# Chunk 0 of a delta-rule attention kernel: where the unread TensorE products stand, at which steps the next chunk's keys are turned, and when the betas are copied

## The chip, the cores and the metric

The kernel runs on one core of a Trainium2 chip. A core has five engines that run side by side, each working through its own list of instructions in order: TensorE (PE in the profile; its weight loads are listed as PEld), VectorE (DVE), ScalarE (ACT), GpSimd (POOL) and SyncE (SP, which here only issues DMAs). Engines wait for one another through semaphores. The metric is the device time of one execution in microseconds (us). A run's time is a little longer than the span that the profile shows, which goes from the first instruction to the last.

## The reference: a delta rule, then a two-layer network

The inputs are q, k and v of shape (4 batches, 8 heads, 768 tokens, 48), and beta of shape (4, 8, 768). Cut to what matters, the reference is:

```python
k_n = k / (np.linalg.norm(k, axis=-1, keepdims=True) + 1e-06)
for t in range(S):
    y[:, :, t] = np.einsum('bhd,bhde->bhe', q[:, :, t], state)
    v_old = np.einsum('bhde,bhd->bhe', state, kt)
    state = state + bt[:, :, :, None] * np.einsum('bhd,bhe->bhde', kt, vt - v_old)
# x: y as (3072 tokens, 384)
h = x @ w_in                       # 384 -> 2048
g = h * (1.0 / (1.0 + np.exp(-h)))
out = g @ w_out                    # 2048 -> 384
```

Every token reads a 48 x 48 state per head, takes out what the state already holds for its key, and adds what is missing. The result goes token by token through a network with a SiLU between two products.

## The kernel before

The 768 tokens are cut into six chunks of 128, and each chunk into halves of 64. Within a chunk the sequential rule becomes products of matrices: the keys' scores against each other, the inverse of a triangular matrix made of them, and products with values, queries and state. All 32 pairs of batch and head are worked on together. The network of the chunks that are done runs on TensorE between the steps of the next chunk, so that TensorE is nearly always busy; only chunk 0 has nothing to run beside it. This case is about the first 50 us, in which chunk 0 is prepared.

**Who sets the order.** The program is one long list in the source. `pin(op)` ties every instruction behind the one before it on the same engine, so each engine runs its instructions in the order in which the source makes them. DMAs on SP are chained by `in_line`. Later loads of weights are held until TensorE reaches certain instructions: `pin` counts TensorE's instructions, and `loads` names the counts.

**The steps of chunk 0, in the order of TensorE.** A "turn" transposes the keys (`turn(c, b, 0, ...)`, b being the batch) or the queries (`turn(c, b, 1, ...)`) of one batch on TensorE with four 128 x 128 transposes (L510); ACT or DVE copies the result out of PSUM (L520 for queries, L524 for keys on ACT, L522 for keys on DVE). `score` multiplies turned keys with turned keys, or with turned queries, in 16 small products of 64 x 64 (L539, two matmul records for each); the copies of its result are L554 on ACT and L557 on DVE. `first_score(b)` are the key scores, `first_queries(b)` the query scores. `beta_of(c)` transposes the betas of one chunk on TensorE (L361) and copies them out on ACT (L364). `diagonal_blocks` copies the blocks of the key scores that are to be inverted (L554 on ACT, L560 on POOL), and `turn_diagonal` transposes them on DVE (L578).

**The chain on DVE.** `norm_steps(0)` computes the inverse lengths of the keys in small steps of DVE (L403 to L426); the step at L420 multiplies them by the betas of chunk 0. `invert_first` then inverts 16 x 16 blocks: a first step (L697) and 15 pairs of steps (L705, L709), each of which is a `next(inv)` in a loop over `n`, and two transposes at the end (L716, L720). The `joins` put the blocks together: `corner` (L743 on TensorE, L750 on DVE), `turned` (L759), `straight` (L772) and `merge_half` (L832). The first product of `corner` waits for L716, and L750 stands behind L720 on DVE.

**The unread products.** `busy(n)` puts n products of the zeroed state with the identity matrix on TensorE (L347, 128 x 384, two matmul records for each product). Nobody reads them. With an instruction and `Sync` given, the first of them waits for that instruction. `busy` and the copies of scores share three PSUM banks in turn.

**Around the change.** Behind the key scores stand the two query turns of batches 0 and 1, one `busy`, the query scores of batch 0, three `busy`, the query scores of batch 1, the transposes of the betas of chunks 1 to 5, two `busy`, the query turns and the query scores of batches 2 and 3. ACT then narrows the first piece of `w_in` (`begin`, L233 and L234). In the loop over `n` stand one `busy` behind each of the steps 0, 1, 2, 4 and 8 and one behind step 15, and the turns of chunk 1's keys at the steps 10, 12, 14 and 15. These turns take their PSUM banks from `M`, which has two, so the third turn waits for ACT's copy (L524) of the first, and the fourth for that of the second. The copies go into `stage`, where the diagonal blocks lay before. After this loop come the joins.

Of the kernel before, what the change touches and what calls it, by code (L numbers as in the profile page):

```python
# [19 lines left out]
def kernel(  # L20
# [37 lines left out]
    A, CC, M = deque(("a0", "a1", "a2")), deque(("c0", "c1", "c2")), deque(("m0", "m1"))  # L58
    kept_banks = {tag: banks.tile([P, 512], FP32, name=f"pb_{tag}", tag=tag) for tag in CC}

    def bank(room, name):

        tag = room[0]
        room.rotate(-1)
        return kept_banks.get(tag) or banks.tile([P, 512], FP32, name=name, tag=tag)

    NoSync, Sync = mybir.DependencyClass.NoSync, mybir.DependencyClass.Sync

    def behind(later, earlier, how=NoSync):

        tc.add_manual_dep(
            later.ins, earlier.ins.name,
            mybir.DependencyInfo(how, mybir.DependencyReason.DATA), reason="order",
        )
# [3 lines left out]
    def pin(op):  # L78

        engine = op.ins.engine  # L80
        if engine in pins:
            behind(op, pins[engine])
        pins[engine] = op
        if engine in tensor[:1]:
            begun[0] += 2 if op.ins.is_transpose else 4
            while loads and begun[0] >= loads[0][0]:
                paced(*loads.popleft()[1:])
        return op
# [254 lines left out]
    def busy(n=1, after=None, how=NoSync, wide=DM):  # L343

        for _ in range(n):
            pw = bank(CC, "pw")
            done = pin(nc.tensor.matmul(  # L347
                pw[:, 0:wide], lhsT=ident[:],
                rhs=states[0][:].rearrange("p u a w -> p (u a w)")[:, 0:wide], start=True, stop=True,
            ))  # L350
            tensor.append(done.ins.engine)
            if after is not None:
                behind(done, after, how)
                after = None
# [4 lines left out]
    def beta_of(c):  # L359
        pb = bank(A, "pb")  # L360
        pin(nc.tensor.transpose(  # L361
            pb[:, 0:BH], beta_fm[:, c].rearrange("n s t -> n (s t)"), ident[0:BH, 0:BH]
        ))
        pin(nc.scalar.activation(  # L364
            out=beta_tok[:, c, :].rearrange("p (n e) -> p e n", e=2),
            in_=pb[:, 0:BH].rearrange("p (e n) -> p e n", e=2), func=ACTF.Copy,
        ))
# [19 lines left out]
    def add_squares(c, b):  # L387

        pin(nc.vector.tensor_reduce(
            out=sums[c][:, b * H : (b + 1) * H], in_=squared[c, b], axis=AX.X, op=ALU.add  # L390
        ))
# [92 lines left out]
    def kq_room(c, b):  # L484

        if c != 1:
            kqs[c, b] = turned_kq[:, b].rearrange("p j a t -> p a j t")
        elif b % HB == 0:
            both = stage[:].rearrange("p (u j a t) -> p u a j t", u=B, a=NP, j=2)
            for u in range(HB):  # L490
                kqs[c, b + u] = both[:, b + u]
# [11 lines left out]
    def turn(c, b, j, room, by_vector=False):  # L503

        if j == 0:
            kq_room(c, b)
        src, kq = (kbufs[c % 2], queries[c] if c < 2 else None)[j][:, b], kqs[c, b]
        pt = bank(room, "pt")
        for p in range(NP):
            pin(nc.tensor.transpose(  # L510
                pt[:, p * C : (p + 1) * C], src[:, p].rearrange("p e w -> p (e w)"), ident[:]
            ))
        ptv = pt[:].rearrange("p (a t) -> p a t", a=NP)
        if j == 1:
            if by_vector:
                pin(nc.vector.tensor_scalar(
                    out=kq[:, :, j, :], in0=ptv, scalar1=-1.0, scalar2=None, op0=ALU.mult
                ))
            else:
                pin(nc.scalar.mul(kq[:, :, j, :], ptv, -1.0))  # L520
        elif by_vector:
            pin(nc.vector.tensor_copy(out=kq[:, :, j, :], in_=ptv))  # L522
        else:
            pin(nc.scalar.copy(kq[:, :, j, :], ptv))  # L524

    def score(c, b, js, rooms, evacuate):

        g, u = b // HB, b % HB
        if (c, g) not in aps:
            aps[c, g] = {}  # L530
        for j in js:
            if j not in aps[c, g]:
                aps[c, g][j] = work.tile([P, HB, H, W], FP32, name=f"ap{j}", tag=f"ap{j}", bufs=2)
        ap, kq, n = aps[c, g], kqs[c, b], len(js)
        pa = [bank(room, f"pa{e}") for e, room in enumerate(rooms)]
        for p in range(NP):
            for e, hf in ((0, 0), (1, 1), (0, 1), (1, 0)):
                rows, half = slice(W * e, W * e + D), slice(W * hf, W * (hf + 1))
                pin(nc.tensor.matmul(  # L539
                    pa[e][half, p * n * W : (p + 1) * n * W], lhsT=kq[rows, p, 0, half],  # L540
                    rhs=kq[rows, p, js[0] : js[-1] + 1, half], start=True, stop=True,
                ))
        for e in range(2):
            of = pa[e][:, 0 : NP * n * W].rearrange("p (a j t) -> p a j t", a=NP, j=n)
            for i, j in enumerate(js):
                evacuate(j, e, ap[j][:, u, e::2, :], of[:, :, i, :])
# [17 lines left out]
    def diagonal_blocks(c, g, engines):  # L564

        if g == 0:
            room = stage if c == 0 else sum_room
            diagonals[c] = room[:, 0 : BH * T].rearrange("p (n t) -> p n t", t=T)
        for j, by in enumerate(engines):
            rows, cols = slice(T * j, T * (j + 1)), slice(T * (j % 2), T * (j % 2 + 1))  # L570
            by(
                diagonals[c][rows, HH * g : HH * (g + 1)],
                aps[c, g][0][rows].rearrange("s u h t -> s (u h) t")[:, :, cols],
            )
# [740 lines left out]
    def first_score(b):  # L1315

        def evacuate(j, e, to, of):
            (by_dve if e else by_act)(to, of)

        score(0, b, (0,), (A, CC), evacuate)  # L1320
# [14 lines left out]
    first_score(1)  # L1335
    first_score(2)
    first_score(3)
    diagonal_blocks(0, 0, (by_pool, by_pool, by_act, by_act))
    diagonal_blocks(0, 1, (by_act, by_act, by_act, by_act))
    add_squares(0, B - 1)  # L1340
    beta_of(0)

    def first_queries(b):

        def evacuate(j, e, to, of):
            by_act(to, of)

        score(0, b, (1,), (A, CC), evacuate)
# [4 lines left out]
    load_v(0)  # L1353
    for b in range(2):
        turn(0, b, 1, M)
    busy(1)
    for _ in norm_steps(0):
        pass
    first_queries(0)
    busy(3)  # L1360
    first_queries(1)
    step = step_of[0]
    of_step = blocks[0][2].rearrange("p s t -> p (s t)")[:, 0 : T * T : T + 1]
# [34 lines left out]

    for n in range(Q):
        done = next(inv)  # L1400
        if n in (0, 1, 2, 4, 8):
            busy(1, done, Sync)
        if n == 10:
            turn(1, 0, 0, M)
        if n == 12:
            turn(1, 1, 0, M)
        if n == 14:
            turn(1, 2, 0, M)
        if n == 15:
            busy(1, done, Sync)  # L1410
            turn(1, 3, 0, M)
    corner, turned, straight = next(inv)
    pin(nc.gpsimd.memset(slab, 0.0))

# [192 lines left out]
    for c in range(1, NCH):  # L1607
# [5 lines left out]
        for word in chunks[c].split():  # L1613
            what, n = word[0], int(word[1:] or 1)
# [55 lines left out]
```

## Time and profile before

| | |
|---|---|
| median of 3 runs | 642.54 us (642.02 to 643.44) |
| the profiled execution's own time | 641.09 us |
| its span | 638.9 us |
| mean granted TensorE clock | 0.987 of full |
| TensorE busy | 621.8 us, 97% of the span |
| VectorE busy | 396.8 us, 62% |
| ScalarE busy | 222.2 us, 35% |
| GpSimd busy | 94.0 us, 15% |

The page divides the span into 40 slices of 16 us. A timeline row gives start, duration, engine, source line, operation, result and operands, size, and how many like instructions it merges; in brackets is the engine's idle time ahead of it and who ended that. The chain is the work that ended last, followed back from the end; "issue" in it is time in which the engine waited for nothing that the profile shows. A row of the table of windows gives a stretch of time, its length, and for each engine the busy time and the number of records in it, then the granted clock of TensorE, the busy share of the DMA engines and GB/s.

### The profile page before, as it was taken

What the parts mean: (1) busy time and instruction counts of PE and PEld (TensorE: products, weight loads), DVE (VectorE), ACT (ScalarE), POOL (GpSimd) and SP (SyncE); (2) the same over time, 40 slices, a digit from 0 to 9 for tenths busy, and PEclk for the clock granted to TensorE, in tenths of its full rate; (3) what the DMA queues carried; (4) which work ended last, traced back from release to release, by engine and by line L of the source; (5) the groups of instructions that cost most, each with busy time, mean ns of one, the idle gap of its engine ahead of it and who ended that gap; (6) DMA issues with size and microseconds to landing.
All of it is one profiled execution on the core that took longest, in us unless ns stands there. A gap on an engine that the chain in (4) does not pass through costs nothing.

```text
span 638.9 us, 21371 instructions
## 1 busy us (share of the span) xinstructions
PE 621.8 (97%) x9406; PEld 546.5 (86%) x9406; DVE 396.8 (62%) x900; ACT 222.2 (35%) x511; POOL 94.0 (15%) x101
## 2 busy tenths in 40 slices
PE   6979999999999999999999999999999999999997
PEld 4678778656799989989989989989889989989997
DVE  6866879999676974546974545975455964112112
ACT  5456883323351122451122451122451122441120
POOL 5223741335020020020020020020002000000000
PEclk9779999999999999999999999999999999999999
DMA  9646606350367450459150359242353133010101
GB/s 174 130 128 176 201 16 149 100 98 4 81 117 169 77 99 12 104 96 193 27 96 16 81 123 161 54 86 26 64 114 79 26 73 37 16 39 1 26 0 26
DMA packets 136940, 52.60 MB, mean 82 GB/s; under 512 B 108672, under 2 KB 130432, under 8 KB 136848
## 3 DMA queue, kind: packets, MB, share of 16 engines
q1 hardware_dynamic: 136512, 51.09, 39.0%
q8 instruction: 74, 1.21, 0.8%
q10 hardware_dynamic: 336, 0.15, 0.1%
q14 instruction: 18, 0.15, 0.1%
HBM read 39.09 MB, written 9.96 MB: 77 GB/s over the span
## 4 chain that ended last, share of the span: by engine, by line
PE 95%; ACT 1%; issue 1%; DMA 1%; DVE 0%; SPq 0%; POOL 0%; POOLq 0%
PE phid L1072 40%; PE px L1189 17%; PE py L1189 13%; PE po L1116 5%; PE pa L539 3%; PE pb_c L866 3%; PE pb_c L854 2%; PE pyc L945 2%; PE pb_c L1116 2%; PE pb_c L886 1%; PE pyc L932 1%; PE pb_c L347 1%; PE px L808 1%; PE py L808 1%; PE pt L510 1%
## 5 line engine op out<-in xcount | busy, mean ns | idle before, releaser
L1072 PE MATMUL phid<-xT,w_in 128*128 128x256 f32 x1152 | 257.1, 381 | 0.2 <-DVE xT L919 0.2
L1072 PEld LDWEIGHTS phid<-xT,w_in 128*128 128x128 f32 x1152 | 216.4, 190 | 30.2 <-issue 0.9
L1082 ACT ACTIVATE gT<-phid 128x512 f32<-128x512 f32 x88 | 52.4, 597 | 142.2 <-PE phid L1072 135.5
L1170 DVE TENSOR_TENSOR sums_of_g<-gT 128x384 f32<-128x384 f32 (+1 forms) x60 | 30.3, 527 | 66.1 <-ACT gT L1082 55.8
L656 DVE SCALAR_TENSOR_TENSOR rank<-g,step,x 128x31 f32<-128x31 f32 (+15 forms) x124 | 49.8, 401 | 22.2 <-DMA g<-blocks 18.7
L1189 PE MATMUL px<-sums_of_w,sums_of_g 128*128 128x192 f32 x320 | 56.6, 329 | 0.0
L1189 PE MATMUL py<-w_out,sums_of_g 128*128 128x192 f32 x320 | 56.2, 328 | 0.0
L1189 PEld LDWEIGHTS px<-sums_of_w,sums_of_g 128*128 128x128 f32 x320 | 52.2, 190 | 0.4
L1189 PEld LDWEIGHTS py<-w_out,sums_of_g 128*128 128x128 f32 x320 | 52.3, 190 | 0.3
L661 DVE TENSOR_TENSOR x<-x,rank 128x31 f32<-128x31 f32 (+15 forms) x124 | 42.5, 343 | 4.3
L477 POOL TENSOR_TENSOR vf<-vf,n_slot 128x768 f32<-128x768 f32 x10 | 14.8, 1492 | 175.0 <-DMA vf<-in_v_dram 120.5
L554 ACT COPY xT<-pyc 48x128 f32<-48x128 f32 (+2 forms) x126 | 32.7, 260 | 1.7
L498 DVE STREAM_TRANSPOSE kq<-stage 128x512 f32<-128x512 f32 x28 | 28.3, 1116 | 5.1 <-DMA xT<-part 3.4
L1189 PE MATMUL py<-w_out,gT 128*128 128x192 f32 x160 | 29.1, 330 | 0.0
L1200 DVE TENSOR_TENSOR o<-o,kept 128x192 f32<-128x192 f32 (+1 forms) x29 | 11.5, 421 | 27.1 <-ACT kept L1197 27.1
L1189 PE MATMUL px<-w_out,gT 128*128 128x192 f32 x160 | 27.9, 327 | 0.0
L1189 PE MATMUL px<-sums_of_w,gT 128*128 128x192 f32 x160 | 27.8, 327 | 0.0
L560 POOL COPY g<-x 64x256 f32<-64x256 f32 x4 | 5.0, 1243 | 150.5 <-DVE x L664 150.5
L1189 PEld LDWEIGHTS px<-w_out,gT 128*128 128x128 f32 x160 | 26.5, 190 | 0.6
L1189 PEld LDWEIGHTS py<-w_out,gT 128*128 128x128 f32 x160 | 26.1, 190 | 0.5
L891 DVE TENSOR_TENSOR state<-state,pb_c 128x384 f32<-128x384 f32 x22 | 11.2, 550 | 24.3 <-PE pb_c L886 24.2
L1189 PEld LDWEIGHTS px<-sums_of_w,gT 128*128 128x128 f32 x160 | 26.2, 190 | 0.1
(232 smaller groups left out, 941.0 us busy)
## 6 DMA issues: line engine op xcount, KB each, us to landing
vf<-in_v_dram SPq DMA_DIRECT2D x48, 96.0 KB, 2.9
out_dram<-o SPq DMA_DIRECT2D x42, 96.0 KB, 2.2
w_out<-in_moe_w_in_dram SPq DMA_DIRECT2D x4, 768.0 KB, 4.8
sums_of_w<-in_moe_w_out_dram SPq DMA_DIRECT2D x4, 768.0 KB, 4.6
kb<-in_k_dram SPq DMA_DIRECT2D x12, 192.0 KB, 4.2
kb<-in_k_dram SPq DMA_DIRECT2D x24, 96.0 KB, 4.1
raw<-in_moe_w_in_dram SPq DMA_DIRECT2D x3, 768.0 KB, 7.1
blocks<-ap SPq DMA_DIRECT2D x32, 64.0 KB, 1.9
```

The lines of the kernel that those rows point to most:

```text
L477: pin(nc.gpsimd.tensor_tensor(out=vf, in0=vf, in1=of, op=ALU.mult))
L498: pin(nc.vector.transpose(out=kqs[c, b][:, :, j, :].rearrange("p a (i m) -> p a m i", i=T), in_=src.rearrange("p a (m d) -> p a m d", d=D) ...
L539: pin(nc.tensor.matmul(pa[e][half, p * n * W : (p + 1) * n * W], lhsT=kq[rows, p, 0, half], rhs=kq[rows, p, js[0] : js[-1] + 1, half], sta ...
L554: return pin(nc.scalar.copy(to, of))
L656: pin(nc.vector.scalar_tensor_tensor(out=tv, in0=g[:, 0:m, m : m + 1].to_broadcast([P, m, n]), scalar=step[:, m : m + 1], in1=x[:, m : m + ...
L661: yield pin(nc.vector.tensor_tensor(out=x[:, 0:m, m:T], in0=x[:, 0:m, m:T], in1=tv, op=ALU.add))
L866: yield pin(nc.tensor.matmul(pz[rows, n * D : (n + 1) * D], lhsT=xis[g][rows, u * H + 2 * p + e, :], rhs=vfs[c][rows, hf, g * HB + u, p, : ...
L1072: pin(nc.tensor.matmul(ph[:, j * GT : (j + 1) * GT], lhsT=w_in[:, a, (2 * f + j) * P : (2 * f + j + 1) * P], rhs=xTs[c, hf][:, a, :], star ...
L1082: pin(nc.scalar.activation(out=hidden_of(c, hf, f), in_=ph[:], func=ACTF.Silu, scale=-0.5 if in_blocks(c) else 0.5))
L1116: pin(nc.tensor.matmul(pos[i][:, 0:DM], lhsT=hidden_of(0, hf, f // 2)[:, at : at + C], rhs=w_outs[f // HFF][:, f % HFF, :], start=(f == 0) ...
L1170: pin(nc.vector.tensor_tensor(out=sums_of_g[:, k, fs], in0=of[0], in1=of[1], op=op))
L1189: pin(nc.tensor.matmul(to, lhsT=at, rhs=quarter(f, *b) if isinstance(b, tuple) else sums_of_w[b][:, f], start=start and f == 0, stop=f == ...
```

## The change

Three things are moved, and nothing is added or taken away.

1. `beta_of(0)` stands ahead of the diagonal copies. On TensorE nothing changes by this; on ACT the copy of chunk 0's betas (L364) comes ahead of six copies of diagonal blocks (L554) instead of behind them.
2. The three `busy` between the query scores of batch 0 and batch 1 stand ahead of both, together with the one that was there.
3. In the loop of the inversion there is no `busy` behind the steps 0, 1, 2, 4, 8 and 15. There are two behind step 9, two behind step 11, one behind step 13 and one behind step 14. The turns of chunk 1's keys stand at the steps 6, 8, 10 and 12 instead of 10, 12, 14 and 15.

The number of `busy` is 15 before and after, and TensorE's instructions from `corner` on keep their places in its list.

```diff
+    beta_of(0)
     diagonal_blocks(0, 0, (by_pool, by_pool, by_act, by_act))
     diagonal_blocks(0, 1, (by_act, by_act, by_act, by_act))
     add_squares(0, B - 1)
-    beta_of(0)
...
     for b in range(2):
         turn(0, b, 1, M)
-    busy(1)
+    busy(4)
     for _ in norm_steps(0):
         pass
     first_queries(0)
-    busy(3)
     first_queries(1)
...
     for n in range(Q):
         done = next(inv)
-        if n in (0, 1, 2, 4, 8):
+        if n in (9, 11, 13):
+            busy(2 if n < 13 else 1, done, Sync)
+        if n in (6, 8, 10, 12):
+            turn(1, n // 2 - 3, 0, M)
+        if n == 14:
             busy(1, done, Sync)
-        if n == 10:
-            turn(1, 0, 0, M)
-        if n == 12:
-            turn(1, 1, 0, M)
-        if n == 14:
-            turn(1, 2, 0, M)
-        if n == 15:
-            busy(1, done, Sync)
-            turn(1, 3, 0, M)
```

## The prediction, made before the changed kernel was run

> **What bounds the kernel now.** The page comes first: its busy times, the slices and the chain.
>
> ```profile
> PE 621.8 (97%) x9406; PEld 546.5 (86%) x9406; DVE 396.8 (62%) x900; ACT 222.2 (35%) x511; POOL 94.0 (15%) x101
> PEclk9779999999999999999999999999999999999999
> PE 95%; ACT 1%; issue 1%; DMA 1%; DVE 0%; SPq 0%; POOL 0%; POOLq 0%
> ```
>
> TensorE is the chain for 95% of the span, and its clock is below full in slices 1 and 2 alone, 16 to 48 us. Behind that it has work without a break, so what is gained or lost ahead of about 50 us should reach the end unchanged. The second view is the chain in order of time, from chunk 0's diagonal copies to the joins.
>
> ```profile
> 15.78 0.49 ACT kq L520
> 16.32 0.36 PE pa L539
> 17.45 4.14 PE pb_c L347 x6
> 22.67 0.63 ACT ap L554 x2
> 26.40 0.27 PE pa L539
> 27.58 0.76 PE pb_c L347 x2
> 28.37 0.93 ACT w_in L233
> 29.30 0.95 ACT raw L234
> 31.52 0.60 ACT stage L524
> 33.47 0.44 PE pt L510 x4
> 33.90 0.14 PE pl L743 x2
> 35.61 0.25 issue
> 37.63 1.96 issue
> 42.07 1.09 issue
> ```
>
> Three unread products (six records, L347) stand between the first two query scores for 4.14 us, on the path. Each stage up to `corner` (L743, about 33.85) follows them. The third view is the table of windows, which tells why they are so slow.
>
> ```profile
> 5.32:8.73 3.41, 2.38 (x43) 1.55 (x42) 1.61 (x3) 1.45 (x3) 1.96 (x3) 1.00 0.91 155
> 12.15:15.56 3.41, 1.04 (x6) 0.42 (x4) 2.81 (x14) 3.33 (x6) 0.55 (x4) 1.00 1.12 293
> 15.56:18.97 3.41, 2.65 (x35) 1.93 (x36) 3.05 (x5) 1.82 (x5) 2.57 (x8) 0.50 0.86 124
> 18.97:22.39 3.42, 3.42 (x37) 1.74 (x35) 2.94 (x13) 0.00 (x0) 0.00 (x0) 0.50 0.97 258
> 36.04:39.45 3.41, 1.59 (x128) 1.48 (x122) 2.74 (x7) 1.62 (x5) 0.83 (x1) 1.00 0.61 162
> 42.87:46.28 3.41, 3.12 (x87) 3.05 (x87) 2.23 (x5) 2.24 (x4) 0.00 (x0) 0.50 0.91 273
> 48.00:50.00 2.00, 2.00 (x62) 1.92 (x60) 1.82 (x3) 0.59 (x2) 0.00 (x0) 0.57 0.05 11
> ```
>
> The clock is 1.00 up to 15.56, 0.50 to 22.39, and 0.50 again from 39.45; the 0.57 of the last row puts the second rise at 49.7. The two spells are 6.8 and 10.2 us, two and three times 3.41, and the falls lie 23.9 us apart, seven times 3.41: the clock changes on a grid of 3.41 us. A window with 1.04 us of work (30%) or 1.59 (47%) was followed by a fall, one with 2.38 (70%) was not. A cold window of 2.65 or of 3.12 us was not followed by a rise, one of 3.42 was.
>
> **The change part by part.** The timeline gives the prices (PE, ACT, DVE).
>
> ```profile
> 12.38 0.81 PE L347 MATMUL pb_c<-state,ident 128*128 128x384 f32 x2
> 17.38 2.93 PE L347 MATMUL pb_c<-state,ident 128*128 128x384 f32 x4
> 23.72 1.56 PE L347 MATMUL pb_c<-state,ident 128*128 128x384 f32 x4
> 22.52 0.31 PE L361 MATMUL pb<-ident,beta_fm 32*128 32x32 f32 x2
> 23.08 0.71 PE L361 MATMUL pb<-ident,beta_fm 32*128 32x32 f32 x3 [0.24 <-ACT ap L554]
> 25.11 1.04 PE L510 MATMUL pt<-ident,z 128*128 128x128 f32 x8
> 11.79 3.76 ACT L554 COPY stage<-ap 32x512 f32<-32x512 f32 x6
> 15.81 0.19 DVE L420 TENSOR_TENSOR nt<-nr,beta_tok 128x32 f32<-128x32 f32 x1 [0.41 <-ACT beta_tok L364]
> 24.18 0.29 DVE L709 TENSOR_TENSOR sums_of_w<-sums_of_w,rank 128x126 f32<-128x126 f32 x1
> 27.84 1.06 DVE L716 STREAM_TRANSPOSE sums_of_w<-sums_of_w 128x512 f32<-128x512 f32 x1
> 34.58 0.34 DVE L750 SCALAR_TENSOR_TENSOR sums_of_w<-pl,second,pick 64x128 f32<-64x128 f32 x1 [3.87 <-PE pb_c L743]
> ```
>
> Betas first: ACT does the same copies before the query turns' copy (L520), so that stays at 15.8 us. DVE no longer waits 0.41 us at L420, and everything behind it on DVE moves up by that: its next input, the diagonal blocks, is done some 0.2 us later, at 15.75, still ahead of DVE, which has two more small steps behind L420 (15.4) and comes to L578 at about 16.0. By itself this is worth nothing at the end, for DVE waits 3.87 us for `corner` at L750; TensorE is the cover.
>
> Four products ahead of the query scores: a product costs 0.78 us warm (1.56 for two) and 1.46 cold (2.93). Four warm ones, 3.1 us from 12.4 on, end at 15.5, inside TensorE's wait for ACT's copy, which ends at 16.27. They cost nothing, and they fill the window that ended at 15.56 with 1.04 us of work, so that the clock should not fall there. The cover is ACT's 3.76 us of copies.
>
> The scores behind them: both batches warm take 1.18 us (26.40 to 27.58, two scores), so they end at about 17.5, where the second ended at 22.6. From there to the end of the fourth took 4.98 us and keeps its parts, but ACT has batch 0's two copies in front of the beta copies now, some 0.1 us. So the fourth ends at 22.6 instead of 27.58.
>
> The inversion's loop: the first two key turns (1.04) end at 23.65; the first two products wait for step 9 (the second row of that shape, done at 24.47, less 0.41: 24.06) and end at 25.6. The third turn waits for ACT. There, from the scores' end at 27.58 to the end of L234 at 30.25 is 2.67 us, and the first L524 takes 0.6: 22.6 + 3.3 = 25.9. A turn (0.52), two products, a turn, two products: 0.52 + 1.56 + 0.52 + 1.56 = 4.2, so `corner` starts at 30.1 instead of 33.85, 3.75 us earlier. The products' waits for steps 11, 13 and 14 are over by then: DVE is done with step 15 ahead of L716, at 27.4. Behind a waiting product stand only turns and `corner`; behind ACT's L524 only the narrowing of the next weights. Next to be late would be L716, at 28.5, and L720 behind it, which has twice its elements and so, by an estimate, ends at 30.6, just clear of L750 (30.8).
>
> SP and POOL keep their lists; the weights' loads hang on TensorE's instructions in the joins and move with them. The key turns now stand at 22.6 rather than 30.84, so chunk 1's keys must have landed.
>
> ```profile
> 10.58 7.80 SPq L144 DMA_DIRECT2D kb<-in_k_dram  x6
> DMA to landing us min/median/max: 4.0/7.2/7.3
> ```
>
> The three loads of batches 0 and 1 are issued by about 14.5 and land by about 22 at the latest; those of the other two, issued by 18.4, by 25.7, ahead of the third turn at 25.9. This is near, and costs at most some tenths.
>
> The joins are not free to follow `corner`. Records done by TensorE, weight loads and matmuls, at the three stalls marked "issue":
>
> ```profile
> 0.00:35.60 35.60, 28.05 (x472) 19.19 (x472) 24.49 (x72) 18.36 (x40) 13.75 (x36) 0.90 0.71 137
> 0.00:37.63 37.63, 29.83 (x600) 20.85 (x600) 25.89 (x76) 19.69 (x42) 15.02 (x36) 0.91 0.68 131
> 0.00:42.07 42.07, 32.31 (x727) 23.19 (x728) 29.34 (x82) 21.39 (x47) 16.85 (x37) 0.89 0.67 136
> ```
>
> That is 944, 1200 and 1455: TensorE runs dry every 256 instructions, so it waits for its own code, and resumes at 35.86, 39.59 and 43.16, 3.7 and 3.6 us apart. These places in its list are the same after the change. The next piece seems to be asked for when TensorE's sequencer enters a piece, here number 688, just behind `corner`'s start at 680; the code came 2.0 us after `corner`. With the same lead it comes at 32.1 (a gain of 3.75). The last wait in front of 688 was ACT's second L524, at 32.6, 3.3 us ahead of 35.86; in the new order it is L716 at 28.5, which gives 31.8 (4.05). Without any lead it would be 30.1 + 3.3 = 33.4 (2.5). I take 3.8, by the row that it is nearest to, the lead as it was, and keep 2.5 and 4.05 for the range. The two later stalls stay as they are.
>
> The Trainium skill, Runtime: NRT & Kernel Launch, section Instruction fetch mechanics, has code refilled in blocks of 256 instructions and calls the cost of crossing a boundary mostly hidden. The block size agrees with 944, 1200 and 1455; the cost does not, with 1.96 and 1.09 us. By the page the gain would be `corner`'s 3.75 us, by the rows 2.5 to 4.05.
>
> The sum: -3.8 us. On the profiled execution (641.09, a span of 638.9 and 2.2 around it) that gives 637.3. Its time lies 1.45 below the median, and I put the sum on the median: 642.54 - 3.8 = 638.7.
>
> **The rivals.** (a) The clock falls once more, at 18.97. The window up to there then has two scores (1.2 us), five beta transposes (0.31 + 0.71) and little else, 2.2 to 2.4 us or 65 to 70%, just at the window that stayed warm. Two products and half of a turn at half clock cost 1.4 + 0.3, less 0.3 of the wait for step 9: 1.4 lost, 640.1. The grid's phase against the start need not be the same in every execution, which speaks for it in some runs.
>
> (b) Slower: the clock falls there and does not come back before the joins. TensorE's work from 18.9 to `corner` is eight products (6.2), six turns (3.1) and two scores (1.2), 10.5 us warm; at 2.93 / 1.56 times that it is 9.3 us longer. Less 0.6 of waits that it swallows and the 3.8 gained it comes to +4.9, 647.4. It decides when no window between 19 and 30 is as full as the one that brought the rise (3.42), since 3.12 did not do. Against it: two products, cold, are 2.9 us on end with turns right behind. The Trainium skill, TensorE: Matmul & The Clock Gate, Part 4, says that transposes do not count as busy in the same way for the clock, which would make this rival likelier and (a) too. The window from 5.32 speaks against the rule here: without its eight transposes (about 1.06 us) it had 1.3 us of work, less than the 1.59 that brought a fall, and stayed warm.
>
> (c) Nothing changes: the joins are held by something that does not move, such as code or weights. For it speaks that 3.6 us between stalls is no matter of TensorE's work; against it that the first of these pieces is asked for by TensorE itself. Price 0: 642.5.
>
> (d) More: with the joins 3.8 us earlier the second cold spell is shorter. The stall of 1.96 us then lies at 33.8 to 35.8, again in one window (32.63 to 36.04), so the clock falls again, at a place 0.4 us later in the work. Since code sets the pace up to 43.16, a warm clock would save at most the two last merges and the first outputs, about 0.9 us: 637.8.
>
> **How the numbers follow.** The forecast, 638.7, has 0.62 with its own range of 637.5 to 640; (a) 0.15, (b) 0.08, (c) 0.07, (d) 0.08. A change of 0.2% (1.3 us) is about what a measurement of this kernel can tell from none. Faster by more are the forecast, (a) and (d): 0.85; same 0.07; slower 0.08. The range goes from 637.0, under (d), to 641.3, over (a) and where faster ends, and leaves out (b), (c) and the forecast's odd ends, under 0.2.
>
> **What would show it.** Right: no idle of 3 us on PE ahead of the query scores, clock 1.00 from 15.56 to 22.39, the second query scores done by 18, `corner` at 30 to 30.5, L420 without a wait on ACT, the code stalls again at 944, 1200 and 1455 with the first resuming at about 32. Wrong: a clock of 0.50 between 19 and 30, a turn of chunk 1 waiting for its DMA, a new "issue" stall between the scores, or the joins starting earlier and the network's first product (L1072) not.

## The result, and the profile after

The changed kernel took 637.95 us (median of 6 runs, 636.44 to 640.07); the kernel before took 642.7 us (6 runs, 642.02 to 643.44) on the same chip. The ratio is 0.9926, with a 95% interval of 0.9907 to 0.9944. On a second chip it was 638.19 against 642.14, 0.9944 (0.9925 to 0.9962). The change makes the kernel 0.6 to 0.7% faster. The forecast was 638.7.

The profiled execution of the changed kernel took 640.07 us, with a span of 637.9: it is the slowest of the six. So its parts are read beside those of a second profiled execution of the same kernel (638.45 us, span 636.3), called "the second execution" below.

The page of the changed kernel, in the lines shown for the one before:

```profile
PE 621.1 (97%) x9406; PEld 546.0 (86%) x9406; DVE 397.5 (62%) x900; ACT 222.1 (35%) x511; POOL 94.0 (15%) x101
PEclk9968999999999999999999999999999999999999
PE 94%; DVE 3%; issue 1%; DMA 1%; ACT 0%; SPq 0%; POOL 0%; DVEq 0%; POOLq 0%
```

The busy times are those of before; nothing was removed. The low clock of slices 1 and 2 has become one of slices 2 and 3. In the chain VectorE has come up from under 1% to 3%, and the chain in order of time shows where:

```profile
12.42 0.19 DVE seed L403
16.21 2.00 DVE sums_of_w L578
18.23 0.70 DVE sums_of_w L697
27.69 1.06 DVE sums_of_w L716
28.75 1.41 DVE sums_of_w L720
30.44 0.31 DVE sums_of_w L750
31.95 0.21 PE pb_c L759
33.28 1.31 issue
37.02 1.41 issue
47.94 1.53 PE phid L1072 x6
50.74 0.44 issue
55.12 1.71 issue
57.08 3.31 PE phid L1072 x9
```

Three readings. First, from 12.4 to 31.9 us the chain is VectorE's: the inverse lengths, the inversion and its transposes. The kernel before had TensorE's unread products and turns here. Second, L750 starts at 30.44 instead of 34.58 (4.1 us earlier), the first product of the network (L1072) at 47.94 instead of 53.03 (5.1 us earlier; 48.39 in the second execution, 4.6 earlier). Third, behind that point this execution gives most of it back: it stops for code at 50.74 and 55.12, and the wide products behind take 3.31 us for nine records.

The timeline of the changed kernel, for the rows on which the prediction was built:

```profile
12.45 2.75 PE L347 MATMUL pb_c<-state,ident 128*128 128x384 f32 x8
24.37 1.56 PE L347 MATMUL pb_c<-state,ident 128*128 128x384 f32 x4 [0.72 <-DVE sums_of_w L709]
25.77 0.61 PE L510 MATMUL pt<-ident,kb 128*128 128x128 f32 x4
29.33 0.20 PE L743 MATMUL pl<-sums_of_w,ap 32*32 32x16 f32 x2
15.58 0.23 DVE L420 TENSOR_TENSOR nt<-nr,beta_tok 128x32 f32<-128x32 f32 x1
```

The four products ahead of the query scores end at 15.2, inside TensorE's wait; `corner` starts at 29.33; L420 no longer waits for ScalarE. And the table of windows, on this execution's grid of 3.41 us:

```profile
13.51:16.92 3.41, 2.21 (x40) 1.20 (x40) 2.96 (x12) 3.26 (x6) 1.47 (x8) 1.00 1.16 224
16.92:20.33 3.41, 2.97 (x55) 2.06 (x48) 3.10 (x8) 1.77 (x9) 1.48 (x2) 1.00 0.69 125
30.57:33.99 3.42, 2.31 (x141) 1.93 (x133) 2.94 (x8) 1.40 (x4) 2.85 (x2) 1.00 0.36 75
40.81:44.23 3.42, 3.42 (x84) 3.42 (x84) 3.26 (x6) 0.48 (x1) 0.00 (x0) 0.50 0.46 85
57.88:61.30 3.42, 3.42 (x10) 2.44 (x8) 0.00 (x0) 0.00 (x0) 0.30 (x1) 0.50 0.33 125
```

The clock stays at 1.00 from 6.7 to 33.99; it is 0.50 to 44.23, and again from 57.88 to 61.30, right behind the stall of 1.71 us.

### The profile page after: what moved, and what is told of

It is laid out like the page before. It is cut to its first block, busy times and chain, and to the rows that moved or that the text cites. A ratio compares the mean times of both kernels' runs of the same rounds, so it can differ in the third digit from the quotient of the medians.

```text
span 637.9 us, 21370 instructions
## 1 busy us (share of the span) xinstructions
PE 621.1 (97%) x9406; PEld 546.0 (86%) x9406; DVE 397.5 (62%) x900; ACT 222.1 (35%) x511; POOL 94.0 (15%) x101
## 4 chain that ended last, share of the span: by engine, by line
PE 94%; DVE 3%; issue 1%; DMA 1%; ACT 0%; SPq 0%; POOL 0%; DVEq 0%; POOLq 0%
PE phid L1072 40%; PE px L1189 17%; PE py L1189 13%; PE po L1116 5%; PE pb_c L866 3%; PE pa L539 3%; PE pb_c L854 2%; PE pyc L945 2%; PE pb_c L1116 2%; PE pb_c L886 1%; PE pyc L932 1%; PE px L808 1%; PE py L808 1%; PE pb_c L539 1%; PE pt L510 1%
## 5 line engine op out<-in xcount | busy, mean ns | idle before, releaser
L1072 PE MATMUL phid<-xT,w_in 128*128 128x256 f32 x1152 | 258.7, 383 | 1.4 <-issue 1.2
L1072 PEld LDWEIGHTS phid<-xT,w_in 128*128 128x128 f32 x1152 | 217.4, 191 | 31.9 <-issue 2.3
L554 ACT COPY xT<-pyc 48x128 f32<-48x128 f32 (+2 forms) x126 | 32.8, 260 | 1.7
```

What stands on the lines that cost most here:

```text
L554: return pin(nc.scalar.copy(to, of))
L1072: pin(nc.tensor.matmul(ph[:, j * GT : (j + 1) * GT], lhsT=w_in[:, a, (2 * f + j) * P : (2 * f + j + 1) * P], rhs=xTs[c, hf][:, a, :], star ...
```

## The experiments

Twelve kernels were run, the changed one's second execution among them. The table has, for them and for the two profiled executions that stand above: when the clock was low ahead of 30 us; the start of `corner` (L743); the start of the first packet of code for the joins (queue q8, 16 KB, from the trace's list of packets); the times at which TensorE goes on in L832 behind its first and its second stall for code; the time at which the clock is back behind its low spell in the joins; the start of L1072; the profiled execution's time; and the ratio of its kernel's runs to the kernel before, with the interval.

| kernel | clock low | `corner` | first packet | L832 goes on | and again | clock back | L1072 | us | ratio |
|---|---|---|---|---|---|---|---|---|---|
| before | 15.6-22.4 | 33.83 | 33.52 | 39.59 | 43.16 | 49.71 | 53.03 | 641.09 | 1 |
| changed | - | 29.33 | 27.73 | 34.59 | 38.43 | 44.23 | 47.94 | 640.07 | 0.9926 (0.9907-0.9944) |
| changed, second execution | - | 29.74 | 28.18 | 34.58 | 38.42 | 45.32 | 48.39 | 638.45 | 0.9944 (0.9925-0.9962) |
| betas alone | - | 31.17 | 31.08 | 37.42 | 40.99 | 49.33 | 51.68 | 640.03 | 0.9989 (0.9965-1.0013) |
| products alone | - | 29.50 | 29.55 | 35.99 | 39.83 | 47.75 | 50.30 | 637.88 | 0.9947 (0.9922-0.9972) |
| loop alone | 17.4-20.8 | 33.39 | 31.36 | 37.97 | 41.53 | 48.12 | 51.39 | 638.52 | 0.9968 (0.9943-0.9993) |
| changed, three products out | 18.6-22.0 | 31.10 | 30.06 | 36.66 | 40.52 | 45.92 | 49.79 | 640.57 | 0.9966 (0.9942-0.9991) |
| load later | - | 29.10 | 27.79 | 34.68 | 38.53 | 46.54 | 49.04 | 637.13 | 0.9938 (0.9921-0.9956) |
| 72 instructions in, loads at their work | | | | | | | | | 1.0110 (1.0082-1.0139) |
| 72 instructions in, loads counted | - | 29.25 | | | | 46.98 | 49.75 | 646.07 | 1.0092 (1.0061-1.0122) |
| wait last | - | 29.07 | 28.55 | 34.95 | 38.52 | 47.07 | 49.26 | 637.11 | 0.9943 (0.9921-0.9964) |
| products alone, last one free | - | 29.53 | 29.06 | 35.37 | 39.21 | 45.07 | 48.74 | 636.17 | 0.9940 (0.9919-0.9960) |
| both waits out | 19.4-22.8 | 31.30 | 29.19 | 35.79 | 39.36 | 46.66 | 49.52 | 636.36 | 0.9961 (0.9938-0.9984) |
| both waits out, load later | - | 29.24 | 27.54 | 34.40 | 37.96 | 44.38 | 47.75 | 636.18 | 0.9934 (0.9912-0.9956) |

The low spell in the joins was 10.2 us long in some executions and 13.7 us in others (betas alone, products alone, load later, 72 instructions in, wait last). L1072 starts 2.2 to 3.9 us behind its end in every row, so its start carries a difference of the clock as well. The end of the second stall in L832 lies ahead of that.

**One part at a time.** The kernel before with the betas first:

```diff
     first_score(3)
+    beta_of(0)
...
     add_squares(0, B - 1)
-    beta_of(0)
```

> The kernel before with the betas' copy ahead of the diagonal copies, and nothing else. Theory (TensorE sets the joins' start): DVE moves up by 0.3 to 0.4 us, and `corner` stays at 33.8 us, so the time stays at 642.7 us within 0.3. Rival (the chain on DVE sets it): 642.3, and `corner` 0.4 us earlier.

Measured: 641.5 us, ratio 0.9989; no effect that can be told from none. In its profiled execution the clock did not fall ahead of 30 us at all, although TensorE waited as long ahead of the query scores as before (3.13 us, 13.40 to 16.53); the grid lay so that this wait was cut by its line at 15.20. That is why its `corner` is early. It is chance, and the first sign that one execution of this kernel is not like the next. The chance is of use: with the products still between the query scores, the warm clock alone has `corner` at 31.17, 2.7 us ahead of the kernel before.

The kernel before with the products ahead:

```diff
-    busy(1)
+    busy(4)
     for _ in norm_steps(0):
         pass
     first_queries(0)
-    busy(3)
     first_queries(1)
```

> The kernel before with the three unread products moved ahead of the query scores, and nothing else. Theory (this part carries the gain, since the products stood on TensorE's path and the clock fell in the empty wait): clock 1.00 from 15 to 30 us, the second query scores done at 17.6, `corner` at 29.3 to 30.3 us, time 638.3. Rival (each part gives a share; without the new places in the inversion's loop the products there wait for its steps and give most of it back): `corner` at 31.5 or later, time 640 to 641.

Measured: 638.1 us, ratio 0.9947, as the theory had it. By the intervals this cannot be told from the whole change (0.9926 and 0.9944). `corner` starts at 29.50, as in the whole change and 1.7 us ahead of the warm execution with the betas alone; this part is the products' way off the path. Yet L1072 starts at 50.30 instead of 47.94 or 48.39. Its chain tells what is left:

```profile
28.20 1.08 DVE sums_of_w L716
30.95 0.30 DVE sums_of_w L750
33.77 2.22 issue
38.47 1.36 issue
50.30 1.53 PE phid L1072 x6
```

The stall in L832 is 2.22 us where the changed kernel has 1.31. TensorE goes on 1.4 us later than there behind the first stall and behind the second; the other 0.5 to 1.0 us go with the clock, which is back at 47.75 instead of 44.23 or 45.32.

The kernel before with the loop's new places:

```diff
-        if n in (0, 1, 2, 4, 8):
+        if n in (9, 11, 13):
+            busy(2 if n < 13 else 1, done, Sync)
+        if n in (6, 8, 10, 12):
+            turn(1, n // 2 - 3, 0, M)
+        if n == 14:
             busy(1, done, Sync)
...
```

> The kernel before with the new places of products and key turns in the inversion's loop, and nothing else. Theory (TensorE is late there, so the same work in another order takes as long, and the third key turn waits for ScalarE without products to fill it): `corner` at 33.8 to 34.8 us, time 642.7 to 643.7. Rival (the loop's places carry the gain): time 640 or less.

Measured: 639.74 us, ratio 0.9968; faster by 0.3%. The theory had it no faster; the rival's "640 or less" was met, though on this chip the kernel before has a median of 641.54 and not 642.7. `corner` starts only 0.44 us earlier than before, and the clock was low for 3.4 us ahead of it where it was low for 6.8; but the stall in L832 is half as long:

```profile
37.02 0.95 issue
40.40 1.13 issue
51.39 1.53 PE phid L1072 x6
```

So the loop brings something that the start of `corner` does not explain.

The changed kernel without the three products that were moved ahead (a `busy(1)` where it has `busy(4)`; three unread products are left out):

> The changed kernel without the three unread products that it moves, which nobody reads, so TensorE idles from 13.2 to 16.4 us as it did before. All instructions behind them stand 12 places earlier in TensorE's list. Theory (the products are worth their place because they keep the clock up): the clock falls to 0.50 at about 16 us and the scores, the turns and two products run at half speed until about 22, so `corner` comes 1.5 to 3 us later than in the changed kernel, at 31 to 32.5, time 639.5 to 641. Rival (what helps is that they are off the path, the clock plays no part): 637.9 within 0.4.

Measured: 640.3 us, ratio 0.9966. The clock fell at 18.61, one window later than the theory said, and `corner` starts at 31.10, 1.4 to 1.8 us later than in the changed kernel. So what the three products did where they stand now was to keep the clock up, in the executions compared. How much of the 0.2 to 0.4% in the median is the clock's is not shown, for the 12 instructions that are left out also move every later step between pieces of code.

**What the loop brings.** A *piece* below is 256 instructions of TensorE's code, which one packet of 16 KB brings; the *step* is the place in TensorE's list where it goes from one piece to the next. The table's columns for the packet and for the first stall in L832 belong together: in all twelve executions that show both, TensorE goes on 6.1 to 6.9 us behind the first packet (before 39.59 - 33.52 = 6.07; changed 6.86; loop alone 6.61), whatever `corner` does. `corner` to the same point takes 4.5 to 6.5 us. In the changed kernel the packet is 1.6 us ahead of `corner`, in the kernel before 0.3, with the products alone it is 0.05 behind. The view of DMA queues for 27 to 33 us has, in the changed kernel,

```profile
q8 instruction: 2, 0.03, 2.5%
```

and no such row at all in the kernel before. What TensorE waits for in L832 is the packet behind this one: it goes on 2.4 to 3.0 us behind that second packet in all twelve, and the second starts 3.4 to 4.2 us behind the first and 0.5 to 1.6 us behind TensorE's step at record 944. Which of the two holds it is not told by this.

What lets the first packet go? In all twelve it starts 0.9 to 1.5 us behind the end of the last wait that stands 17 or more TensorE records ahead of the step to the next 256: with the products alone this is the unread product that waits for the step n = 15 (28.17, packet 29.55); in the changed kernel the one that waits for n = 13 (26.71, packet 27.73; second execution 27.11 and 28.18). Three runs were made to try this. The first moves that wait back in the changed kernel:

```diff
-        if n in (9, 11, 13):
-            busy(2 if n < 13 else 1, done, Sync)
+        if n in (9, 11):
+            busy(2, done, Sync)
...
-        if n == 14:
+        if n == 15:
             busy(1, done, Sync)
+            busy(1, done, Sync)
```

> The changed kernel with the two unread products behind the turns of chunk 1's keys waiting for the step with n = 15 of the inversion (its end was 27.66 us) instead of n = 13 (26.71) and n = 14 (27.21). `corner` comes behind them on TensorE as before and waits for VectorE's transpose until 28.75 anyway. Theory (the first piece of code for the joins is asked for when the last wait that stands 17 or more instructions ahead of the step between pieces lets go, and TensorE goes on in L832 6.1 to 6.9 us after that piece's packet, so the loop's new places are worth what they bring this wait forward): packet at 28.7 to 29.0 us instead of 27.73 and 28.18, end of the stall in L832 at 35.1 to 35.8 instead of 34.6, first wide product 0.5 to 1.2 us later, median 0.4 to 1.2 us above the changed kernel's. Rival (the start of `corner` and VectorE's steps decide): packet moves or not, stall ends at 34.4 to 34.8 us, median within 0.3 us.

Measured: packet at 28.55, and the chain

```profile
30.20 0.31 DVE sums_of_w L750
33.05 1.90 issue
49.26 1.53 PE phid L1072 x6
```

The packet is later by 0.4 to 0.8 us and the stall ends at 34.95 (0.36 later), though `corner` and L750 are the earliest of all: both in the theory's direction, by less than it said. But TensorE passed the step at record 944 at 31.01, ahead of the changed kernel's two executions (31.24 and 31.68), so the later packet had still come in time. By the end of the second stall 0.1 us is left (38.52 against 38.43). L1072 starts 0.9 to 1.3 us later, but the clock came back later too, at 47.07; the run with the load later, whose front is the changed kernel's own, has 46.54 and 49.04. The median, 637.15 us, ratio 0.9943, is no higher than the changed kernel's. So this run shows that the wait moves the packet, and not that the packet's delay costs anything; the total speaks for the rival. Behind the front this execution stops less than the second one does: 0.68 us at 84 against 1.32, 0.28 at 445 against 0.56, and not at 543, where that one has 0.31.

The second takes the wait away from the kernel with the products alone:

```diff
         if n == 15:
-            busy(1, done, Sync)
+            busy(1)
             turn(1, 3, 0, M)
```

> The kernel before with the products ahead alone (betas and loop as before), and the unread product of n = 15 not waiting for its step. In the run with the products ahead its wait let go at 28.17 us and the packet came at 29.55; behind it the next wait, on ScalarE's copies, lets go at 27.86. Theory: packet at 28.7 to 29.1 us, end of the stall in L832 at 35.1 to 35.7 us instead of 35.99, median 0.3 to 0.9 us below that run's (ratio to the kernel before about 0.994 instead of 0.9947). Rival (the wait has nothing to do with the code): packet at 29.4 to 29.7 us, stall ends at 35.9 to 36.1, ratio as in that run.

Measured: packet at 29.06, and

```profile
31.14 0.30 DVE sums_of_w L750
33.97 1.40 issue
48.74 1.53 PE phid L1072 x6
```

The stall ends at 35.37, 0.62 us earlier, with `corner` where it was. Packet and stall lie as the theory said. The second stall ends 0.62 us earlier too, at 39.21, where the changed kernel is at 38.43; this is 0.6 of the 1.4 us that the loop brings there. L1072 starts 1.56 us earlier, but 0.9 of this stands behind the second stall, where the clock was back at 45.07 instead of 47.75. The median is 636.38 us, ratio 0.9940, against 0.9947: the same to within the intervals.

The third takes both waits away from the changed kernel (`busy(1)` for n = 13 and n = 14), and the fourth puts the load of the next part beside it:

> The changed kernel with the two unread products of n = 13 and n = 14 not waiting for their steps. The wait ahead of them, on ScalarE's copies, let go at 26.16 us in its profile. Theory: first packet at 27.2 to 27.6 us; the second packet is held by TensorE's way through `turned` (30.9 us), so the stall in L832 ends only 0 to 0.5 us earlier, 34.1 to 34.7 us; median within 0.5 us of the changed kernel's, rather below. Rival (the packet alone paces the joins): stall ends at 33.7 to 34.1 us.

> As the run without the two waits, and the load of weights behind 50 us put 75 TensorE instructions later as in its own run (637.64 us against 638.19). If the two add: about 637.4 us, 0.9925 to 0.9935 of the kernel before; if neither does anything: 638.2 us, 0.994.

Measured: 637.59 us, ratio 0.9961, and 636.61 us, ratio 0.9934. In the first the clock fell at 19.35, so its times in the front cannot be compared; its packet at 29.19 stands 1.1 us behind ScalarE's copies (28.12), as the theory has it. In the second the packet is at 27.54, 0.2 us ahead of the changed kernel, and the stall ends at 34.40, also 0.2 ahead, both where the theory had them without the waits. Its ratio is the one said for the two adding, but its interval holds the other value as well. Neither is a version that can be told from the changed kernel.

**The stalls behind 50 us.** The changed kernel again, beside the next three:

> The changed kernel again, on the chip of the next three runs, to have them compared with it. Every theory: about 638 us, 0.993 of the kernel before. The code stalls of the profiled execution before (1.31 and 1.41 us in the first joins, 0.44 and 1.71 us at 50.7 and 55.1 us) should come back at the same instructions, whatever the phase of the clock; if the 1.71 us does not, it was chance.

Measured: 638.19 us, ratio 0.9944. Its chain:

```profile
33.90 0.64 issue
37.22 1.21 issue
48.39 1.53 PE phid L1072 x6
55.15 0.34 issue
55.73 2.79 PE phid L1072 x12
```

The two stalls in the first joins are there again; the 1.71 us at 55.12 is a 0.34, and there is no cold spell behind it. It was chance, by the rule set before the run. In the first execution a 768 KB load of weights had been issued just ahead of TensorE's step to its next 256 instructions:

```profile
50.77 0.37 SPq L292 DMA_DIRECT2D w_out<-in_moe_w_in_dram  x1
```

TensorE stopped there until 51.18 because that piece was itself late, and the packet asked for next started only at 54.57. In the second execution the same load was issued at 51.22 and the step was at 51.20; the packet started at 52.33. The next run moves the load:

```diff
-        (WINDOW + PACKET * 7 + -15, fetch_w_in, 5),
+        (WINDOW + PACKET * 7 + 60, fetch_w_in, 5),
```

> The load of expert weights that SyncE issued at 50.77 us is put 75 TensorE instructions later; nothing else is changed. Theory (this load, asked for just ahead of TensorE's step into its next 256 instructions, holds up that step's own request for code: packet at 54.57 us, 3.4 us after the step, then 1.71 us of stall, then a cold spell of 3.41 us): the packet comes within 1.5 us of the step, the stall at 55.1 us goes, the wide product that took 4.47 us for 12 takes 2.8 again, and the median is 0.5 to 1.7 us below that of the changed kernel run beside it. Rival (the packet was late by itself): stall of 1.5 to 1.9 us at the same place, median within 0.4 us.

Measured: 637.64 us, ratio 0.9938; packet 1.1 us behind the step, no stall at that place. But ten of twelve executions, most with the load where it was, have the packet 0.8 to 1.1 us behind the step too; it was 1.5 us with the wait last and 3.4 us in the changed kernel's first execution alone. That the load held the packet up is likely from its order there, but was seen once, and the gain of 0.55 us against the second execution's kernel is inside the intervals. It stays open.

**Where the pieces of code begin.** The changed kernel with 18 small unread products behind the four, in the 1.2 us that TensorE waits there:

```diff
     busy(4)
+    for _ in range(18):
+        pw = bank(CC, "pw")
+        done = pin(nc.tensor.matmul(
+            pw[0:T, 0:T], lhsT=ident[0:T, 0:T], rhs=ident[0:T, 0:T], start=True, stop=True,
+        ))
+        tensor.append(done.ins.engine)
+        begun[0] -= 4
```

> 18 unread 32x32 products (72 TensorE instructions) are put behind the four that stand ahead of the query scores, inside the 1.2 us that TensorE waits there; the loads keep their places among the work. Theory (code comes in pieces of 256 instructions, and each piece is asked for at the step into the one before it): all stalls lie 72 instructions earlier in the work. The step that sat just behind the first corner product now sits inside it and is taken about 1 us earlier, so the first stall shrinks from 1.31 to 0 to 0.4 us and stands in the first straight products; the second stays, 1.3 to 1.9 us; first joins done 0.5 to 1.2 us earlier. The step near 50 us now comes ahead of the weights' load, so the 1.71 us stall goes too. Median 0.7 to 2.5 us below the changed kernel's. Rival (the stalls belong to the work at those places, not to the count of instructions): both stall at the same products as before, by the same amounts, median within 0.4 us.

and the same without the last line, so that the loads move too:

> As the run with 18 small products, but they count for the loads' triggers, so each load of weights is issued 72 instructions earlier in the work, at its old distance from the steps between pieces of code. Theory (load just ahead of the step delays the code): joins as in that run, but the stall behind the load that now comes at about 49 us is there again, 0.5 to 1.8 us, 72 instructions earlier in the work than in the changed kernel; median 0.3 to 1.5 us above that run's. Rival (loads do not matter to the code): no stall there, median equal to that run's within 0.4 us.

Measured: 649.2 us, ratio 1.011 (1.0082 to 1.0139), and 646.53 us, ratio 1.0092 (1.0061 to 1.0122). Both are slower than even the kernel before, by 8 to 11 us against the changed kernel. None of the theories had that. The second, for which the theory of the loads had 0.3 to 1.5 us more than the first, took 2.7 us less. The rows are from the second of the two; the first's profiled execution, 656.92 us, lies above its five other runs (646.03 to 651.57) and is left out. The stalls stand at the same counts of instructions as ever, and so 72 instructions earlier in the work: the first is in L772 (0.71 us), the second in L832 (1.62), as said, which settles that the count decides and not the work. The start of L1072 did not gain from it (49.75). No stall came at 49 us, which speaks against the theory of the loads too. Most of the loss lies far behind:

```profile
343.27 2.12 issue
435.35 1.90 issue
550.69 1.50 issue
```

The windows around the first of them, in this kernel and then in the changed one's second execution (up to the stall, a window holds a part of the work that is 3.7 us further on in the latter):

```profile
340.00:344.00 4.00, 3.27 (x198) 3.06 (x198) 1.68 (x3) 0.93 (x3) 0.00 (x0) 1.00 0.01 4
```

```profile
340.00:344.00 4.00, 4.00 (x129) 3.77 (x130) 2.85 (x6) 1.57 (x4) 0.00 (x0) 1.00 0.02 4
```

At 343 us the shifted kernel had a whole piece of 256 filled with small products (198 matmul records in the window), ran through it in less time than the next takes to come, and stopped. The piece ended 3.40 us after it began (341.98 to 345.38); at 435 and 550 us it was 3.62 and 3.74. Matched instruction by instruction against the second execution, the shifted kernel lies 2.6 us behind at 100 us and 3.2 at 250; behind the three stalls it is 5.8 (at 340), 7.6 (at 430) and 7.7, which stays to the end.

## Why the prediction was right, point by point

**Betas first, worth nothing.** Right by itself (0.9989). But the cover that it named, TensorE, is gone in the whole change: the chain from 12.4 to 31.9 is VectorE's. There the 0.41 us of wait at L420 shortens the way from the last sum of squares (L389) to L716 from 16.1 to 15.8 us. So up to 0.3 us of the front hangs on it; that was not measured alone.

**Four products ahead, free, and the clock stays up.** Right: end at 15.2, scores behind them warm, clock 1.00 to 33.99, second query scores done at 17.58 (forecast 17.5) and fourth at 22.62 (22.6).

**The loop.** `corner` at 29.33 where 30.1 was forecast. The third turn started at 25.77 (forecast 25.9); the 4.2 us from there measured 3.56. The step summed 0.52 for a turn and 1.56 for two products, which counts the end of each that overlaps the next.

**Next to be late: L716 and L720.** Right, and already so: L720's last step in the chain ends at 30.16 and L750 follows at 30.44, 1.1 us behind `corner`; in the kernel before it followed at 0.75.

**The code behind `corner`, "with the same lead".** This step failed. The lead grew from 0.3 to 1.6 us, because L716 (done at 28.75) does not hold the packet (27.73): the waits 17 or more records ahead do. TensorE did not stop for code at 944 at all. "The two later stalls stay as they are" failed with it: they were 1.31 and 1.41 us long instead of 1.96 and 1.09, and the first ended 5.0 us earlier (34.59 against 39.59), the second 4.7 (38.43 against 43.16). At L1072 the gain was 5.1 us (4.6 in the second execution) and not 3.8. The Trainium skill, Runtime: NRT & Kernel Launch, Instruction fetch mechanics, has the next block fetched while the current one runs, at a cost that is mostly hidden. The first half agrees with a packet that comes ahead of `corner`; the second does not hold here, with 0.6 to 2.2 us for a boundary among small products.

**"What is gained ahead of about 50 us should reach the end unchanged".** For single executions this failed: of 5.1 us at L1072, 1.0 is left in the span, in the second execution 2.6 of 4.6. The rest goes in stalls for code and in spells of the clock that differ from one execution to the next. But the profiled execution of the kernel before, 641.09 us, was faster than all six of its runs above, and that of the changed kernel was the slowest of its six. By the medians 4.75 us of the 5.1 are left, and on the second chip 3.95 of the 4.6; so most of the gain reaches the end, and what is lost is not measured well. That the forecast lies 0.75 us from the median is in part luck: 1.3 us more came at L1072 than it had, something was lost behind that, and the median of the kernel before itself differs from chip to chip (642.7, 642.14, 641.54, 641.12).

**The rivals.** (a), one more cold spell, did not come in the changed kernel's two profiled executions; the run with both waits out shows it at 19.35 to 22.77, with the same four products ahead. (d): the second cold spell did fall again, at 33.99, and was 10.2 us long as before. (c) was half right: the joins are paced by code, but the code moved. (b), the slow side: in the three comparable executions where the clock fell in the front (loop alone, three products out, both waits out) it was back 3.4 us later.

**The threshold of the clock.** The prediction set it between 47% and 70% of a window. Three windows, of the runs with the betas alone, without the three products, and with both waits out:

```profile
11.79:15.20 3.41, 1.61 (x10) 0.99 (x10) 3.00 (x14) 3.34 (x7) 0.69 (x2) 1.00 1.09 293
```

```profile
15.19:18.61 3.42, 1.66 (x67) 1.38 (x67) 3.17 (x7) 3.07 (x11) 2.94 (x9) 1.00 1.00 136
```

```profile
15.94:19.35 3.41, 2.15 (x70) 1.82 (x71) 3.23 (x5) 2.93 (x12) 2.64 (x8) 1.00 0.83 126
```

The first (47%, ten wide records) was not followed by a fall; the second (49%) and the third (63%, nearly all of it scores of 64 x 64) were. So busy time alone does not decide; small products seem to count for less. That was not tested. The Trainium skill, TensorE: Matmul & The Clock Gate, Part 4, has transposes not counted as busy in the same way. The first window speaks against it: eight of its ten records are transposes, and the two others, one unread product of 0.81 us, are what the window that brought the fall in the kernel before had beside transposes too. It is one execution.

## What to carry to other kernels

Put unread work that is to hold the clock into a wait that is there anyway, not between two steps of the path; here that was worth 0.5%. In a long unrolled program of small products, read the stalls by their count of instructions: if they lie 256 apart, as here, look for what each piece of code waits for. A wait well ahead of the step between pieces can hold the packet; here taking one away shortened the front by 0.6 us, and no median shows it. Any edit that adds or removes instructions shifts every later step between pieces, so price it over the whole program, and judge it by several executions.

## What the runs showed of the hardware that was not expected

- 72 instructions that take no time where they stand cost 8 us (646.53 against 638.19), most of it by three stalls for code of 1.5 to 2.1 us, the last some 530 us later.
- A piece of 256 TensorE instructions ran in no less than 3.4 us where it was short of work (3.40, 3.62, 3.74); the packet started 0.4 to 1.7 us behind the step in nine of ten cases between 30 and 60 us, and where TensorE had stopped it went on 2.3 to 3.3 us behind the packet.
- The clock's grid of 3.41 us lies at another phase in each execution. The same wait of 3.1 us brought a fall in the kernel before and none with the betas alone; 30 of 31 runs of the kernel before on one chip spread from 637.9 to 644.2 us.
